# Batch order, one DMA per tensor and batch into 256-byte rows, and weights staged in the second batch's buffers, in a gated linear attention with a max-out layer

## Chip, cores, metric

One core of one Trainium2 chip. The metric is the device time of one execution in microseconds (us), lower is better. Executions of a program on one core carry a state: slow where the run is more than 1.5% above the fastest of the same kernel.

## The reference

```python
batch, n_heads, seq, head_dim = (4, 8, 768, 48)      # q, k, v, f_logit: float32
f = 1.0 / (1.0 + np.exp(-f_logit))
for t in range(S):
    state = f[:, :, t, :, None] * state + np.einsum('bhd,bhe->bhde', k[:, :, t], v[:, :, t])
    y[:, :, t] = np.einsum('bhd,bhde->bhe', q[:, :, t], state)
x = np.ascontiguousarray(y.transpose(0, 2, 1, 3)).reshape(B * S, H * D)     # 3072 x 384
h1 = x @ w1                                          # 384 x 1024
h2 = x @ w2
out = np.maximum(h1, h2) @ w_out                     # 1024 x 384
```

A head's row of 48 floats is 192 bytes in memory, and the rows of one head and batch follow each other. Whatever a load looks like, it is made of runs of 192 B on the memory side.

## The kernel before

A batch's 768 positions are cut into 6 chunks of 128, so there are 24 tiles (4 batches x 6 chunks), taken chunk by chunk: chunk 0 of all batches, then chunk 1, and so on. Four tiles make a group for the second layer. Work of step i is interleaved with "units" of the second layer: `u_d` (matmul d, then Relu) and `u_o` (matmul o, then the copy `ob` and the output DMA).

```python
loads = ctx.enter_context(tc.tile_pool(name="loads", bufs=5))
...
def load(i):
    c, b = divmod(i, B)
    sl = slice(c * C, (c + 1) * C)
    t = {}
    for name, src in (("f", f_logit), ("k", k), ("q", q), ("v", v)):
        t[name] = loads.tile([C, H, D], F32, name=f"{name}t", tag=f"{name}t")
        nc.sync.dma_start(out=t[name], in_=src[b, :, sl, :].rearrange("h p d -> p h d"))
    ld[i] = t
...
for i in range(3):
    load(i)
nc.sync.dma_start(out=w2_f, in_=...)      # 1.5 MB each
nc.sync.dma_start(out=wo_f, in_=...)
load(3)
nc.sync.dma_start(out=w1_f, in_=...)
load(4)
...
ob = work.tile([C, dm], F32, name="ob", tag="ob", bufs=3)
nc.vector.tensor_copy(ob, ps)
nc.sync.dma_start(out=out[r0:r0 + C, :], in_=ob)
...
for i in range(-4, T):
    if i >= 0:
        s_y(i)            # state and y of tile i
    unit()
    if 0 <= i + 2 < T:
        s_tr(i + 2)       # transposes of k', q', copy trs
    unit()
    if 0 <= i + 1 < T:
        s_a(i + 1)        # scores and mask (am)
    unit()
    if 0 <= i + 3 < T:
        s_cum(i + 3)      # cumulative log gates, exp, k' and q' on GpSimd
    unit()
    if i >= 0:
        s_xT(i)
    ...
    if i >= 0 and i % B == B - 1:
        push_group(i // B)
    if 0 <= i + 4 < T:
        s_ell(i + 4)      # reads f, casts v (vb)
    if 5 <= i + 8 < T:
        load(i + 8)
```

## Time and profile before

| | before |
|---|---|
| time, median of 2 runs | 186.99 us (186.93 to 187.04) |
| span of the profiled execution | 183.6 us |
| TensorE busy | 138.6 us (75%) |
| first d matmul of groups 0, 1, 2 | 59.22, 81.98, 104.27 us |
| DMA packets (page, part 3) | 105,154 |

How to read it: the span's last two thirds are set by TensorE, and the second layer's matmuls run in program order, so the starts of the groups' first d matmuls on TensorE's timeline tell where time was lost: each delay stays to the end. A timeline line gives start and length in us, engine, line, operation and tiles, and in brackets the engine's idle time before it with what ended it. A window line gives the stretch and its length, the busy us (and counts) of TensorE, its weight loads, VectorE, ScalarE and GpSimd, then the granted clock, the DMA share and GB/s. A packet is one piece of a DMA as the profile records it; where the DMA share is above 1, the records of one engine's packets overlap in time.

### The profile page before, as it was taken

The numbers are of one execution on the slowest core, as the hardware profiler recorded it, in microseconds if no ns is written. First come the engines' busy times: TensorE is split into PE (matmuls) and PEld (weight loads), VectorE is DVE, ScalarE is ACT, GpSimd is POOL, SyncE is SP. The second block draws the span as 40 slices with busy tenths as digits, with TensorE's granted clock in tenths as the row PEclk, the third lists the DMA queues.
The fourth block names the chain that finished last, engine by engine and source line by source line (L and its number), as shares of the span: only waits on it lengthen the run. The fifth ranks groups of instructions, "written<-read, shape, count | busy, mean of one in ns | idle before, by whom it ended". The sixth has DMA issues, their size and how long they took to land.

```text
span 183.6 us, 3633 instructions
## 1 busy us (share of the span) xinstructions
PE 138.6 (75%) x1373; PEld 85.4 (46%) x1384; DVE 102.5 (56%) x161; ACT 86.1 (47%) x200; POOL 75.7 (41%) x107
## 2 busy tenths in 40 slices
PE   0000208946778989999999998999899988998992
PEld 0000106534555545655456654665556654564560
DVE  8200605389777576686676676766776744452031
ACT  2000074483555675446744577346873376412700
POOL 8200004646666366544466544566544644000000
PEclk9999999985555999999999999999999999999999
DMA  6999999999999997698996999969801120022022
GB/s 114 194 185 347 373 199 362 186 187 171 194 189 190 164 191 131 165 209 174 195 151 164 215 172 186 172 142 216 152 0 43 50 86 0 4 87 86 0 89 86
DMA packets 105154, 28.56 MB, mean 156 GB/s; under 512 B 100272, under 2 KB 104368, under 8 KB 105136
## 3 DMA queue, kind: packets, MB, share of 16 engines
q1 hardware_dynamic: 105136, 28.32, 77.1%
q8 instruction: 11, 0.18, 0.5%
q14 instruction: 7, 0.06, 0.1%
HBM read 23.59 MB, written 4.72 MB: 154 GB/s over the span
## 4 chain that ended last, share of the span: by engine, by line
issue 39%; PE 32%; POOL 23%; ACT 3%; POOLq 1%; DVE 1%; ACTq 0%
PE o L172 13%; POOL qp L221 11%; POOL kp L220 9%; PE d L156 9%; PE tr L230 6%; PE a L245 2%; POOL st L98 1%; ACT ei L216 1%; PE y L272 1%; ACT ed L217 1%; PE y L277 1%; ACT gT L158 1%; POOLq L345 1%; POOL ell L94 0%; PE cum L208 0%
## 5 line engine op out<-in xcount | busy, mean ns | idle before, releaser
L220 POOL TENSOR_TENSOR kp<-kt,ei 128x384 bf16<-128x384 f32 x24 | 24.9, 1036 | 76.4 <-issue 38.9
L156 PE MATMUL d<-xT,wd 128*128 128x512 bf16 x133 | 36.7, 383 | 2.3 <-DVE xT L291 1.1
L158 ACT ACTIVATE gT<-d 128x512 bf16<-128x512 f32 x48 | 29.0, 605 | 19.0 <-PE d L156 18.5
L172 PE MATMUL o<-wo,gT 128*128 128x384 bf16 x192 | 37.7, 326 | 0.0
L234 DVE COPY trs<-tr 128x1024 bf16<-128x1024 bf16 x24 | 16.6, 692 | 25.8 <-PE tr L230 25.7
L248 DVE TENSOR_TENSOR am<-a,mask 128x1024 bf16<-128x1024 f32 x24 | 29.3, 1219 | 2.9 <-PE a L245 2.9
L216 ACT ACTIVATE ei<-cum 128x384 f32<-128x384 f32 x24 | 11.7, 489 | 38.2 <-PE cum L210 38.2
L221 POOL TENSOR_TENSOR qp<-qt,ed 128x384 bf16<-128x384 f32 x24 | 27.6, 1148 | 0.0
L176 DVE COPY ob<-o 128x384 f32<-128x384 f32 x24 | 13.4, 558 | 23.3 <-PE o L172 22.4
L172 PEld LDWEIGHTS <-gT 128*128 128x128 bf16 x192 | 17.8, 98 | 10.4
L267 POOL TENSOR_TENSOR st<-tmp,fl 64x192 bf16<-64x192 f32 x40 | 20.0, 501 | 2.3 <-DVE tmp L264 0.8
L124 PE MATMUL w2tp<-ident,w_h 128*128 128x128 bf16 x24 | 3.5, 308 | 21.0 <-DVE w_h L112 21.0
L201 DVE CAST vb<-vt 128x384 bf16<-128x384 f32 x24 | 16.9, 703 | 0.0
L156 PEld LDWEIGHTS <-wd 128*128 128x128 bf16 x144 | 11.8, 98 | 10.8 <-issue 2.3
L172 PE MATMUL o<-w2o,xT 128*128 128x384 bf16 x72 | 15.7, 327 | 0.0
L230 PE MATMUL tr<-ident,qp 128*128 128x128 bf16 x96 | 10.6, 239 | 5.8 <-POOL qp L221 5.0
L277 PE MATMUL y<-vb,am 128*128 128x48 bf16 x192 | 12.0, 190 | 2.2 <-DVE am L248 1.4
L116 ACT CAST wo<-wo_f 128x768 bf16<-128x768 f32 x4 | 3.1, 824 | 21.9 <-DMA wo_f<-in_moe_w_out_dram 21.9
L208 PE MATMUL cum<-ell,ut 128*128 128x384 bf16 x24 | 8.9, 369 | 6.0 <-ACT ell L199 6.0
L277 PEld LDWEIGHTS <-am 128*128 128x128 bf16 x192 | 10.3, 101 | 6.4 <-DVE xT L291 3.7
L280 ACT CAST x<-y 128x384 bf16<-128x384 f32 x24 | 11.2, 467 | 4.2 <-PE y L277 4.1
L199 ACT ACTIVATE ell<-e 128x384 bf16<-128x384 f32 x24 | 12.5, 523 | 0.9
(42 smaller groups left out, 185.1 us busy)
## 6 DMA issues: line engine op xcount, KB each, us to landing
ft<-in_f_logit_dram SPq DMA_DIRECT2D x24, 192.0 KB, 4.3
kt<-in_k_dram SPq DMA_DIRECT2D x24, 192.0 KB, 4.2
qt<-in_q_dram SPq DMA_DIRECT2D x24, 192.0 KB, 4.2
vt<-in_v_dram SPq DMA_DIRECT2D x24, 192.0 KB, 4.3
out_dram<-ob SPq DMA_DIRECT2D x24, 192.0 KB, 2.0
w_f<-in_moe_w_dram SPq DMA_DIRECT2D x2, 1536.0 KB, 7.7
wo_f<-in_moe_w_out_dram SPq DMA_DIRECT2D x1, 1536.0 KB, 11.0
```

The source lines that it names most:

```text
L156: nc.tensor.matmul(out=ps, lhsT=wd[:, j, f * C:(f + 1) * C], rhs=xT[:, j, :], start=(j == 0), stop=(j == JG - 1))
L158: nc.scalar.activation(gT[:, f, :], ps, AF.Relu)
L172: nc.tensor.matmul(out=ps, lhsT=mms[n][0], rhs=mms[n][1], start=(n == 0), stop=(n == len(mms) - 1))
L201: nc.vector.tensor_copy(vb, t["v"].rearrange("p h d -> p (h d)"))
L216: nc.scalar.activation(ei, ps[:, 0:dm], AF.Exp)
L220: nc.gpsimd.tensor_mul(kp[:, :, 0:D], t["k"], ei.rearrange("p (h d) -> p h d", h=H))
L221: nc.gpsimd.tensor_mul(qp[:, :, 0:D], t["q"], ed.rearrange("p (h d) -> p h d", h=H))
L230: nc.tensor.transpose(out=ps[:, n, p, :], in_=src[:, 2 * p:2 * p + 2, :].rearrange("p h d -> p (h d)"), identity=ident)
L234: nc.vector.tensor_copy(tr, ps)
L248: nc.vector.tensor_mul(am.rearrange("p o n c -> p (o n) c"), ps.rearrange("p o n c -> p (o n) c"), mask)
L267: nc.gpsimd.tensor_mul(new[r, :, e], tmp[r, :, e], s["fl"][r, :].unsqueeze(2).to_broadcast([DP, NP, D]))
L277: nc.tensor.matmul(out=y[:, ds], lhsT=am[:, o, p, :], rhs=vb[:, ds], start=(c == 0), stop=(c == 0 or o == 1))
```

## The change

Its intent: fewer and larger loads. Tiles go batch by batch. The first batch is still loaded tile by tile; from the second on, one DMA per tensor brings all six tiles (1.18 MB). Rows of 192 B are put every 256 B, which makes a buffer 12,288 B a partition, just what a weight matrix in float32 needs; so the three weight matrices are staged in the second batch's buffers.

```diff
-    loads = ctx.enter_context(tc.tile_pool(name="loads", bufs=5))
+    lb = {n: [consts.tile([C, H, nch, DP], F32, name=f"{n}b{x}") for x in range(2)] for n, _ in SRC}   # DP = 64
     def load(i):
-        c, b = divmod(i, B)
+        b, c = divmod(i, nch)
...
+            nc.sync.dma_start(out=lb[name][b % 2][:, :, c, 0:D],
+                              in_=src[b, :, sl, :].rearrange("h p d -> p h d"))
+    def load_batch(b, names):
+        for name, src in SRC:
+            if name in names:
+                nc.sync.dma_start(out=lb[name][b % 2][:, :, :, 0:D].rearrange("p h c d -> p (h c) d"),
+                                  in_=src[b].rearrange("h (c p) d -> p (h c) d", c=nch))
-    w1_f = consts.tile([C, JG, d_ff], F32, name="w1_f")
+    w1_f = lb["f"][1].rearrange("p h c d -> p (h c d)").rearrange("p (j f) -> p j f", j=JG)
     ... (w2_f in lb["k"][1], wo_f in lb["q"][1])
     load(4)
+    load(5)
...
-        if 5 <= i + 8 < T:
-            load(i + 8)
+        if i == 0:
+            load_batch(1, "fkqv")
+        if i >= 0 and i % nch == 1 and i // nch + 2 < B:
+            load_batch(i // nch + 2, "fv")
+        if i >= 0 and i % nch == 2 and i // nch + 2 < B:
+            load_batch(i // nch + 2, "kq")
```

The rest of the diff follows the new order of tiles in the state, the groups and the output rows.

More of the change, by code (lines that the diff above doesn't have):

```diff
@@ L54, with loaded @@
     nc.scalar.preload_act_table_set("natural_log_exp_and_others")
-    ld = {}
+    SRC = (("f", f_logit), ("k", k), ("q", q), ("v", v))
+    lb = {n: [consts.tile([C, H, nch, DP], F32, name=f"{n}b{x}") for x in range(2)] for n, _ in SRC}
     def load(i):
-        c, b = divmod(i, B)
+        b, c = divmod(i, nch)
         sl = slice(c * C, (c + 1) * C)
-        t = {}
-        for name, src in (("f", f_logit), ("k", k), ("q", q), ("v", v)):
-            t[name] = loads.tile([C, H, D], F32, name=f"{name}t", tag=f"{name}t")
-            nc.sync.dma_start(out=t[name], in_=src[b, :, sl, :].rearrange("h p d -> p h d"))
-        ld[i] = t
-    w1_f = consts.tile([C, JG, d_ff], F32, name="w1_f")
-    w2_f = consts.tile([C, JG, d_ff], F32, name="w2_f")
-    wo_f = consts.tile([C, FG, dm], F32, name="wo_f")
+        for name, src in SRC:
+            nc.sync.dma_start(out=lb[name][b % 2][:, :, c, 0:D],
+                              in_=src[b, :, sl, :].rearrange("h p d -> p h d"))
+    def load_batch(b, names):
+        for name, src in SRC:
+            if name in names:
+                nc.sync.dma_start(out=lb[name][b % 2][:, :, :, 0:D].rearrange("p h c d -> p (h c) d"),
+                                  in_=src[b].rearrange("h (c p) d -> p (h c) d", c=nch))
+    def loaded(i, name):
+        b, c = divmod(i, nch)
+        return lb[name][b % 2][:, :, c, 0:D]
+    w1_f = lb["f"][1].rearrange("p h c d -> p (h c d)").rearrange("p (j f) -> p j f", j=JG)
+    w2_f = lb["k"][1].rearrange("p h c d -> p (h c d)").rearrange("p (j f) -> p j f", j=JG)
+    wo_f = lb["q"][1].rearrange("p h c d -> p (h c d)").rearrange("p (j f) -> p j f", j=FG)
     for i in range(3):
@@ L176, in u_o @@
                 nc.vector.tensor_copy(ob, ps)
-                r0 = b * S + g * C
+                r0 = (g * B + b) * C
                 nc.sync.dma_start(out=out[r0:r0 + C, :], in_=ob)
@@ L194, in s_ell @@
     def s_ell(i):
-        t = ld[i]
+        b, c = divmod(i, nch)
+        t = {n: loaded(i, n) for n in "fkqv"}
         e = work.tile([C, dm], F32, name="e", tag="e")
         ell = ell_b[i % 2]
-        nc.scalar.activation(e, t["f"].rearrange("p h d -> p (h d)"), AF.Exp, scale=-1.0)
+        nc.scalar.activation(e.rearrange("p (h d) -> p h d", h=H), t["f"], AF.Exp, scale=-1.0)
         nc.scalar.activation(ell[:, :, 0:D], e.rearrange("p (h d) -> p h d", h=H), AF.Ln, bias=1.0)
         vb = work.tile([C, dm], BF16, name="vb", tag="vb", bufs=6)
-        nc.vector.tensor_copy(vb, t["v"].rearrange("p h d -> p (h d)"))
+        nc.vector.tensor_copy(vb.rearrange("p (h d) -> p h d", h=H), t["v"])
         st[i] = {"ell": ell, "v": vb}
     def s_cum(i):
-        s, t = st[i], ld[i]
+        b, c = divmod(i, nch)
+        s = st[i]
+        t = {n: loaded(i, n) for n in "fkqv"}
         ell = s["ell"]
@@ L222, in s_cum @@
         s.update(fl=fl, qp=qp, kp=kp)
-        del ld[i]
     def s_tr(i):
@@ L252, in s_y @@
     def s_y(i):
-        c, b = divmod(i, B)
+        b, c = divmod(i, nch)
         s = st[i]
@@ L283, in s_xT @@
     def s_xT(i):
-        c, b = divmod(i, B)
+        b, c = divmod(i, nch)
         s = st.pop(i)
-        if b == 0:
-            xT_g[c] = work.tile([C, JG, GT], BF16, name="xT", tag="xT", bufs=3)
+        g, n = divmod(i, B)
+        if n == 0:
+            xT_g[g] = work.tile([C, JG, GT], BF16, name="xT", tag="xT", bufs=3)
         ps = ps_s.tile([C, JG, C], BF16, name="xtp", tag="s")
@@ L290, in s_xT @@
             nc.tensor.transpose(out=ps[:, j, :], in_=s["x"][:, j * C:(j + 1) * C], identity=ident)
-        nc.vector.tensor_copy(xT_g[c][:, :, b * C:(b + 1) * C], ps)
+        nc.vector.tensor_copy(xT_g[g][:, :, n * C:(n + 1) * C], ps)
     for i in range(-4, T):
```

## The prediction

> **What bounds the kernel now.** I read the page's forty slices first, then a table of windows, then the timelines of single engines.
>
> ```profile
> PE   0000208946778989999999998999899988998992
> PEclk9999999985555999999999999999999999999999
> DMA  6999999999999997698996999969801120022022
> GB/s 114 194 185 347 373 199 362 186 187 171 194 189 190 164 191 131 165 209 174 195 151 164 215 172 186 172 142 216 152 0 43 50 86 0 4 87 86 0 89 86
> ```
>
> A slice is 4.6 us. Three stages show. Up to about 40 us the DMA engines are full and TensorE waits for weights and first tiles. From 40 to 60 us TensorE is half busy at half clock. From 60 us on it is at nine tenths, to the end. The DMA row is nearly full until about 130 us, which looks like a bound, but the windows (engine busy times, then granted clock, DMA share, GB/s) say otherwise:
>
> ```profile
> 5.00:10.00 5.00, 0.00 (x0) 0.00 (x0) 0.89 (x1) 0.00 (x0) 0.61 (x2) 1.00 1.31 192
> ...
> 45.00:50.00 5.00, 4.06 (x48) 3.01 (x47) 3.92 (x7) 2.73 (x9) 3.53 (x5) 0.50 1.01 190
> ...
> 85.00:90.00 5.00, 4.32 (x51) 2.53 (x50) 3.22 (x6) 4.12 (x10) 3.04 (x4) 1.00 1.17 196
> ...
> 135.00:140.00 5.00, 4.70 (x57) 2.93 (x55) 3.39 (x6) 3.21 (x8) 3.04 (x4) 1.00 0.00 0
> ```
>
> With no DMA at all (135 to 140 us) TensorE is as busy as with it. The q, k, v, f tiles move at about 190 GB/s wherever they move alone, so the four tiles of a step, 786,432 bytes, take 4.14 us, and a step takes longer: on VectorE's timeline the casts of v (vb) are 4.5 us apart from 45 to 54 us,
>
> ```profile
> 40.06 1.33 DVE L119 TENSOR_TENSOR wd<-w_f 128x1024 bf16<-128x1024 f32 x1
> ...
> 44.95 0.95 DVE L201 CAST vb<-vt 128x384 bf16<-128x384 f32 x1
> ...
> 49.46 0.95 DVE L201 CAST vb<-vt 128x384 bf16<-128x384 f32 x1
> ...
> 53.97 0.96 DVE L201 CAST vb<-vt 128x384 bf16<-128x384 f32 x1
> ```
>
> and later four steps take 22.3 us (output copies below: 72.89 to 95.17). So loads are hidden now. The 45-to-60 us stage is one latency loop (cum, exp, two GpSimd products, transpose); there is no projection work yet, for the first group of four tiles is pushed only after step 3. From its first d matmul (59.22 us on TensorE's timeline) TensorE sets the end: what delays that matmul delays the end by as much.
>
> **What the Trainium skill says.**
> 1. "DMA: Bandwidth & Descriptors", section "Why small descriptors are slow (HBM only)": each packet pays a fixed overhead. The trace agrees: the median packet takes 15 ns for 192 B, 65 ns for 1536 B, 159 ns for 4096 B, about 8 ns plus size. 192 B / 15 ns x 16 engines is 205 GB/s, near the 190 seen. The changed kernel moves the same 98,304 packets of 192 B.
> 2. The same page, "How a descriptor splits into AXI transactions": a start off a 256 B boundary costs beats. The new rows start on one in SBUF, not in HBM. The fit above already explains 15 ns without such a penalty, so I give alignment little.
> 3. The same page, "Why a DMA increments its semaphore by 16 and not by 1": only the full count says that all data has landed. So nobody can use the first tile of a batch DMA before its last has come. No trace of the kernel before can show it, since there each tile had a DMA of its own.
> 4. "TensorE: Matmul & The Clock Gate", Part 1: half clock after idle windows, full clock after about 3.4 us of sustained work. Agrees: 0.5 from 40 to 60 us, and full clock from 60.7 us, 1.5 us after dense work began.
>
> **The change, part by part.**
> *Fewer issues.* 96 input DMAs become 24 small and 12 of 1.18 MB. Issues run on SyncE's queue and are waited for by nobody but transfers; DMAs of 192 KB already stream at 190 GB/s. Gain: 0.
> *Order.* The six tiles of a batch follow each other, so the state of step i is needed in step i+1, not i+4. In the kernel before, in steady state, the state product ends at 106.37 us and the next step's first use is at 109.04 us: 2.7 us of slack. The same numbers of state products and y matmuls exist. Cost: 0.
> *Staging.* The weights' loads come in the same order at the start; load(5) is issued at the same place, now without waiting for a free buffer. Gain 0. But f of batch 1 goes where w1 lay, so in the built program its DMA waits for the last wd subtraction, which ends at 40.06 + 1.33 = 41.4 us. Before, the seventh tile was being issued from 36.9 us.
> *First stall.* Batch 1 comes as f, k, q, v, 4 x 1,179,648 B = 4.72 MB, at 190 GB/s 24.8 us. The shortest landing of a 192 KB tile is 2.7 us, of which 1.03 is transfer, so latency is 1.7 us. v lands at 41.4 + 1.7 + 24.8 = 67.9 us. Step 2 casts v of the seventh tile, at 53.97 us before: VectorE, in order, stands 13.9 us. Behind that cast it still has to do vb 0.35, tmp 0.55, trs 0.69, am 1.22, xT 0.35, then d starts: 71.3 us in place of 59.22. **Cost 12.1 us**, all on the path.
> *Clock.* The stall leaves TensorE cold; dense work then runs at half clock for 3 to 7 us in place of 1.5. About **1.5 us**.
> *Second stall.* Outputs share the queue with the batches and have three buffers (ob):
>
> ```profile
> 72.89 0.56 DVE L176 COPY ob<-o 128x384 f32<-128x384 f32 x1
> ...
> 81.11 0.56 DVE L176 COPY ob<-o 128x384 f32<-128x384 f32 x1 [0.80 <-PE o L172]
> ...
> 95.17 0.56 DVE L176 COPY ob<-o 128x384 f32<-128x384 f32 x1
> ...
> 103.40 0.56 DVE L176 COPY ob<-o 128x384 f32<-128x384 f32 x1 [0.80 <-PE o L172]
> 103.87 0.35 DVE L291 COPY xT<-xtp 128x384 bf16<-128x384 bf16 x1
> ```
>
> In the built program batch 3's four DMAs stand between outputs 4 and 5 on SyncE. In the old times, output 4 is copied at 81.11, f of batch 3 issues at 82.1, q lands 1.7 + 24.8 later at 108.6, output 5 behind it at about 109.2. Output 8, due at 103.40, reuses output 5's buffer, so VectorE waits 5.8 us, and behind it xT of step 11, which the next group's d needs. **Cost 5.8 us**, and about **1 us** of clock. For batch 2 the same sum just fits: it lands at 67.9 + 24.8 = 92.7, output 1 at 93.2, and output 4 is due at 81.11 + 13.6 = 94.7.
> Sum: 187.0 + 12.1 + 1.5 + 5.8 + 1.0 = 207.4; I say 207.
>
> **The rivals.**
> (a) *Aligned rows or large DMAs stream faster.* At 230 GB/s batch 1 needs 20.5 us: v at 63.6, d 7.8 us late, the second stall 1.5 us, clock 1.5: 198 us. For it: the skill's alignment section, and its advice of at least 1 MiB per DMA. Against: the packet fit, and 190 GB/s with small DMAs queued. At the 373 GB/s of the weights there would be almost no stall: 188 to 190.
> (b) *Only the first stall.* If output 5 slips past batch 3, or if f of batch 3 starts early: 200 to 201 us. For it: the ring's depth is not in the profile. Against: one queue, in order.
> (c) *The shorter state loop becomes the bound.* If GpSimd's products came late, each of 20 state steps could lose up to 1 us: up to 20 us more. Against: the slack of 2.7 us.
> (d) *Freed DMA time helps.* It cannot shorten a TensorE-bound second half: windows without DMA are no faster. About 187.
>
> **Range and chances.** 207 if both stalls come in full; (a) in part or (b) gives 198 to 201; slower transfers, with 5% less rate costing 1.3 us in each stall, or a colder clock, give 212. Range 198 to 212. Faster would need a gain that no view shows: 0.02. Within 2% needs nearly the weights' rate: 0.05. Slower: 0.93.
>
> **What would show it.** The DMA groups should list 24 small and 12 large loads, the large ones streaming at 185 to 195 GB/s; v of batch 1 landing near 68 us and VectorE's cast of it waiting some 14 us for that DMA; the first d near 71 us with PEclk at five tenths beyond 70; output 8's copy waiting some 6 us for an output DMA. From there steps of 5.6 us again. The prediction is wrong if the batches stream well above 190 GB/s, if no wait ends on v of batch 1, or if the steady step is not 5.6 us.

## The result, and the profile after

222.75 us (median of 2 runs, 222.57 to 222.92) against 186.99: slower, ratio 1.191 (95% interval 1.186 to 1.196). Ratios here are the mean time of one kernel's fast runs over that of the other's of the same rounds, so not quite the ratio of the medians quoted. The range of the prediction ended at 212: the direction was right, the size wrong.

The slices of the kernel after (5.5 us each):

```profile
PE   0000169468700088995699970689998999999893
PEclk9999999955555569999589995599999999999999
DMA  8999999979999999999599989200210012002012
GB/s 123 163 172 393 256 324 173 107 133 163 163 168 163 163 163 166 163 166 179 150 159 167 167 150 186 100 0 0 74 71 3 0 73 76 0 3 106 36 39 107
```

TensorE has three holes that were not there before, and each is followed by slices at half clock. The rate row is the surprise: where it read 185 to 195 before, it reads about 163, and it does so from the second slice on, while loads are still made tile by tile. The windows of the kernel after say the same (engine busy times, then granted clock, DMA share, GB/s):

```profile
5.00:10.00 5.00, 0.00 (x0) 0.00 (x0) 0.91 (x1) 0.00 (x0) 0.64 (x2) 1.00 1.53 164
...
65.00:70.00 5.00, 0.00 (x0) 0.00 (x0) 0.00 (x0) 0.00 (x0) 0.00 (x0) 0.50 0.94 165
...
85.00:90.00 5.00, 4.21 (x40) 2.08 (x39) 2.82 (x4) 3.89 (x9) 1.76 (x2) 1.00 1.06 166
...
150.00:155.00 5.00, 4.70 (x54) 2.89 (x52) 3.39 (x7) 3.06 (x8) 3.04 (x4) 1.00 0.00 0
```

From 65 to 70 us no engine works and the DMA engines move 165 GB/s: the core waits for data. From 150 us on it works as before.

VectorE's timeline after, the lines that answer to those of before (last wd subtraction, casts of v):

```profile
42.78 1.33 DVE L129 TENSOR_TENSOR wd<-fb,kb 128x1024 bf16<-128x1024 f32 x1
...
47.68 0.95 DVE L212 CAST vb<-vb 128x384 bf16<-128x384 f32 x1
...
52.19 0.95 DVE L212 CAST vb<-vb 128x384 bf16<-128x384 f32 x1
...
76.31 0.36 DVE L212 CAST vb<-vb 128x384 bf16<-128x384 f32 x1 [19.53 <-DMA vb<-in_v_dram]
```

The seventh tile's cast of v, at 53.97 us before, starts at 76.31 after a wait of 19.5 us for the batch's v: the predicted stall, larger. And the output copies:

```profile
105.70 0.56 DVE L186 COPY ob<-o 128x384 f32<-128x384 f32 x1 [4.86 <-DMA out_dram<-ob]
...
138.91 0.56 DVE L186 COPY ob<-o 128x384 f32<-128x384 f32 x1 [9.45 <-DMA out_dram<-ob]
139.38 0.35 DVE L304 COPY xT<-xtp 128x384 bf16<-128x384 bf16 x1
```

These are outputs 4 and 8. Each waits for a buffer whose output DMA stands behind batch loads on SyncE's queue (issue times; the last line is the first of the outputs behind q of batch 3):

```profile
106.84 0.71 SPq L70 DMA_DIRECT2D fb<-in_f_logit_dram  x1
108.00 6.01 SPq L70 DMA_DIRECT2D vb<-in_v_dram  x1
114.47 6.85 SPq L70 DMA_DIRECT2D kb<-in_k_dram  x1
121.77 7.80 SPq L70 DMA_DIRECT2D qb<-in_q_dram  x1
129.67 88.69 SPq L188 DMA_DIRECT2D out_dram<-ob  x20
```

The first d matmul of each group puts the loss in place. The lines of group 0 before, then of groups 0, 1 and 2 after, where TensorE itself waited 4.2 and 9.0 us for an xT copy behind a waiting output copy:

```profile
59.22 0.60 PE L156 MATMUL d<-xT,wd 128*128 128x512 bf16 x1
```
```profile
79.49 1.46 PE L166 MATMUL d<-xT,wd 128*128 128x512 bf16 x3
...
106.58 1.44 PE L166 MATMUL d<-xT,wd 128*128 128x512 bf16 x3 [4.17 <-DVE xT L304]
...
139.78 1.44 PE L166 MATMUL d<-xT,wd 128*128 128x512 bf16 x3 [8.96 <-DVE xT L304]
```

| first d of group | before | after | delay added since the last |
|---|---|---|---|
| 0 | 59.22 | 79.49 | 20.3 us |
| 1 | 81.98 | 106.58 | 4.3 us |
| 2 | 104.27 | 139.78 | 10.9 us |
| end of span | 183.6 | 220.8 | 1.7 us |

The sum is the 37.2 us between the spans.

What the loads are made of has changed too. Part 3 of the page, before:

```profile
DMA packets 105154, 28.56 MB, mean 156 GB/s; under 512 B 100272, under 2 KB 104368, under 8 KB 105136
```

and after:

```profile
DMA packets 48897, 28.54 MB, mean 129 GB/s; under 512 B 25584, under 2 KB 48112, under 8 KB 48880
```

The batch DMAs are recorded as 18,432 packets of 768 B, four rows each, where the tile loads have one packet a row. I had said the packets would stay the same.

### The profile page after: what moved, and what is told of

Same layout as the page of the kernel before. It is cut to its first block, busy times and chain, and to the rows that moved or that the text cites. A ratio compares the mean times of both kernels' runs of the same rounds, so it can differ in the third digit from the quotient of the medians.

```text
span 220.8 us, 3530 instructions
## 1 busy us (share of the span) xinstructions
PE 145.7 (66%) x1384; PEld 87.6 (40%) x1384; DVE 101.4 (46%) x161; ACT 86.5 (39%) x200; POOL 75.5 (34%) x107
## 3 DMA queue, kind: packets, MB, share of 16 engines
HBM read 23.59 MB, written 4.72 MB: 128 GB/s over the span
## 4 chain that ended last, share of the span: by engine, by line
PE 33%; issue 19%; DMA 17%; POOL 14%; SPq 10%; ACT 4%; DVE 2%; POOLq 0%; DVEq 0%; ACTq 0%
PE o L182 12%; PE d L166 11%; SPq L70 10%; DMA out_dram<-ob 9%; DMA vb<-in_v_dram 8%; POOL qp L234 6%; POOL kp L233 5%; PE tr L242 4%; PE a L257 3%; ACT ei L229 3%; POOL st L108 1%; ACT gT L168 1%; PE y L284 1%; DVE ob L186 1%; PE y L289 1%
## 5 line engine op out<-in xcount | busy, mean ns | idle before, releaser
L233 POOL TENSOR_TENSOR kp<-kb,ei 128x384 bf16<-128x384 f32 x24 | 24.9, 1039 | 84.7 <-ACT ei L229 76.4
L166 PE MATMUL d<-xT,wd 128*128 128x512 bf16 x144 | 41.6, 410 | 14.1 <-DVE xT L304 13.9
L234 POOL TENSOR_TENSOR qp<-qb,ed 128x384 bf16<-128x384 f32 x24 | 27.1, 1129 | 0.0
L212 DVE CAST vb<-vb 128x384 bf16<-128x384 f32 x24 | 15.8, 658 | 19.5 <-DMA vb<-in_v_dram 19.5
L166 PEld LDWEIGHTS <-wd 128*128 128x128 bf16 x144 | 12.4, 102 | 24.2 <-issue 16.4
L182 PEld LDWEIGHTS <-gT 128*128 128x128 bf16 x192 | 17.8, 97 | 10.4
L134 PE MATMUL w2tp<-ident,w_h 128*128 128x128 bf16 x24 | 3.5, 308 | 22.3 <-DVE w_h L122 22.3
L272 PE MATMUL sa<-vb,kp 128*128 128x96 bf16 x80 | 7.3, 220 | 16.3 <-DVE tmp L276 15.5
L242 PE MATMUL tr<-ident,qp 128*128 128x128 bf16 x96 | 11.3, 251 | 6.2 <-POOL qp L234 5.6
L209 ACT ACTIVATE e<-fb 128x384 f32<-128x384 f32 x24 | 13.0, 541 | 0.0
```

Of the source, the lines that this page charges most:

```text
L166: nc.tensor.matmul(out=ps, lhsT=wd[:, j, f * C:(f + 1) * C], rhs=xT[:, j, :], start=(j == 0), stop=(j == JG - 1))
L182: nc.tensor.matmul(out=ps, lhsT=mms[n][0], rhs=mms[n][1], start=(n == 0), stop=(n == len(mms) - 1))
L212: nc.vector.tensor_copy(vb.rearrange("p (h d) -> p h d", h=H), t["v"])
L233: nc.gpsimd.tensor_mul(kp[:, :, 0:D], t["k"], ei.rearrange("p (h d) -> p h d", h=H))
L234: nc.gpsimd.tensor_mul(qp[:, :, 0:D], t["q"], ed.rearrange("p (h d) -> p h d", h=H))
L242: nc.tensor.transpose(out=ps[:, n, p, :], in_=src[:, 2 * p:2 * p + 2, :].rearrange("p h d -> p (h d)"), identity=ident)
```

## The experiments

Twelve kernels ran, all correct. Each ran beside the kernel before on the same chip, whose medians in the four calls were 186.84, 186.03, 185.44 and 186.39 us.

The question: why 163 GB/s in place of 190, and is what remains just the two kinds of stall?

### a1_pitch48: no gaps between the rows

```diff
-    lb = {n: [consts.tile([C, H, nch, DP], ...)]}
+    lb_w = {n: [consts.tile([C, H * nch * DP], ...)]}               # the weights' views, as large as before
+    lb = ... lb_w[n][x][:, 0:H * nch * D] seen as [C, H, nch, D]    # rows every 192 B
```

> The changed kernel with the gaps taken out: rows of 192 B stand every 192 B in the batch buffers, so a batch DMA writes one contiguous 9216 B run per partition; everything else (order, batch DMAs, staging) as changed. Theory P (the gap between rows is what brought the load rate from 190 down to 163 GB/s): the batches stream at 190 GB/s or more, v of batch 1 lands near 44.2 + 1.7 + 24.8 = 70.7 us at the latest in place of 76.2, the output waits shrink from 14.3 us to about 6, and the time is 205 to 212 us. Theory Q (a DMA of a whole batch is slow by itself, whatever it writes to): still about 163 GB/s and 220 to 223 us.

206.32 us (203.96 to 207.29, 4 runs), ratio of fast runs 1.096 (1.083 to 1.108). The profiled run is a slow one (207.04), so I take from it only rates (from a5's below, slow too, rates and waits): 216 GB/s from 5 to 10 us, 212 from 50 to 55. So the batch DMA is not slow by itself; where its rows go decides.

### b1_pitch256, b2_pitch208, b3_order: one part each, in the kernel before

```diff
-        t[name] = loads.tile([C, H, D], F32, ...)
+        t[name] = loads.tile([C, H, 64], F32, ...)[:, :, 0:D]     # b1: rows every 256 B; b2: 52, every 208 B
```
```diff
-        c, b = divmod(i, B)                                       # b3, in load, s_y, s_xT, with the output rows
+        b, c = divmod(i, nch)
```

> The kernel before with one thing changed: its 96 tile loads write rows of 192 B every 256 B. Theory P: tiles move at about 163 GB/s in place of 190 from the first slice on (4.8 us a step, still less than the 5.6 us step, so hidden later); weights arrive about 2.7 us later, and the time is 189 to 191 us. Theory Q: 190 GB/s and 187 us as before.

> The kernel before with rows of 192 B every 208 B: a gap, but not the 256 B step. If any gap is what costs (the contiguous run of 1536 B a partition is broken up), 163 GB/s and 189 to 191 us as with 256 B. If it is the step of 256 B itself, 190 GB/s and 187 us.

> The kernel before with the order of tiles alone changed to batch by batch; 96 tile loads into five contiguous buffers as before. My theory: the state product has 2.7 us of slack before the next step's use, so 187 us, within 0.5%. Rival: the state loop of one step binds, each of 20 state steps loses up to 1 us, 190 to 205 us.

b1: 188.20 us, a little under the 189 to 191 expected, ratio 1.008 (1.001 to 1.014), and 163 GB/s in the first windows, one of them here:

```profile
5.00:10.00 5.00, 0.00 (x0) 0.00 (x0) 0.00 (x0) 0.00 (x0) 0.90 (x3) 1.00 1.51 163
```

b2: 186.83 us, ratio 1.001 (0.993 to 1.009), at 194 GB/s in the same window: a gap alone costs nothing, so my theory P of the gap fell. b3: 186.69 us, ratio 0.998 (0.990 to 1.007): the shorter state loop is free, as its 2.7 us of slack said, and the order is no part of the loss.

What tells b1 from b2? I looked up where the built programs put the buffers. They start 128 bytes past a multiple of 256 in the kernel after, and 160 past one in the kernel before and in b1. A row of 192 B that starts 128 past a boundary ends at 320: **every row of the "256-byte rows" crosses a 256 B boundary**, and so does every row of b1 (160 to 352). With rows every 192 B, before, the starts go round 160, 96, 32, 224, and three in four cross. In a1 one in two crosses, in b2 two in three (11 of 16 over its two kinds of buffers). The rates fall in that order. Hence theory X, crossings cost, against theory S, a step of 256 B is slow wherever it starts.

### a5_aligned, b4_aligned256, b5_start32: the same steps, shifted

```diff
+    pad = consts.tile([C, 32], F32, name='pad')                   # a5: 128 bytes; the batch buffers move to 0 past 256
     lb = {n: [consts.tile(...
```
```diff
-        ... loads.tile([C, H, 64], F32, ...)[:, :, 0:D]
+        ... loads.tile([C, H * 64 + 64], F32, ...)[:, 24:24 + H * 64] seen as [C, H, 64], [:, :, 0:D]   # b4; b5: 32:32 + H * 64
```

> The changed kernel with one 128-byte tile allocated ahead of the batch buffers. In the built program the eight buffers then start at 0 past a multiple of 256 B in place of 128, so no 192 B row crosses a 256 B boundary of SBUF any more, where in the changed kernel every row does (128 to 320). Theory X (crossings cost): so far the rate falls with the share of crossing rows: 216 to 227 GB/s at one half (a1), 190 at three quarters (before), 163 at all (after, b1, a3). At none I expect 240 to 330 GB/s, v of batch 1 by 59 to 65 us, no wait of an output copy above 1 us, and 189 to 196 us. Theory S (the step of 256 B is slow whatever the start, say because all rows fall on the same part of the memory): still 163 GB/s and 222 us.

> The kernel before with 96 tile loads into rows every 256 B, as b1_pitch256, but starting at 0 past a multiple of 256 B in place of 160: no row crosses. Theory X: 240 to 330 GB/s in the first 10 us in place of b1's 163 and before's 190; as loads are hidden later, only the start gains: 183 to 186 us. Theory S: 163 GB/s and 188 us, as b1.

> As b4_aligned256, but the rows start at 32 past a multiple of 256 B (32 to 224): no row starts on the boundary and none crosses one. If crossing is what costs, the rate of b4: 208 to 227 GB/s in the first 10 us, nearly all packets at 15 ns, 184 to 187 us. If a start off the boundary costs by itself, less: 163 to 195 GB/s.

Windows of b4, of b5, then of a5 (5 to 10 us, tile loads; 50 to 55 us, batch loads):

```profile
5.00:10.00 5.00, 0.00 (x0) 0.00 (x0) 0.89 (x1) 0.00 (x0) 0.61 (x2) 1.00 1.05 208
```
```profile
5.00:10.00 5.00, 0.00 (x0) 0.00 (x0) 0.91 (x1) 0.00 (x0) 0.63 (x2) 1.00 1.02 205
```
```profile
5.00:10.00 5.00, 0.00 (x0) 0.00 (x0) 0.90 (x1) 0.00 (x0) 0.62 (x2) 1.00 1.06 210
50.00:55.00 5.00, 4.11 (x49) 3.03 (x46) 2.81 (x5) 2.78 (x8) 3.52 (x6) 0.50 0.91 258
```

| rows that cross | kernels | tile loads, 5 to 10 us | batch loads, 50 to 55 us | median batch packet (768 B) |
|---|---|---|---|---|
| all | after, b1, a3 (below) | 164, 163, 164 GB/s | 163 GB/s (after) | 79 ns |
| 3 in 4 | before, b3 | 192, 189 | | |
| 11 in 16 | b2 | 194 | | |
| 1 in 2 | a1 | 216 | 212 | 47 ns |
| none | a5, b4, b5 | 210, 208, 205 | 258 (a5) | 42 ns |

Theory S is out: same step of 256 B, another start, 208 in place of 163 GB/s. The share of 192 B packets over 20 ns goes from 48% (b1) to 0.6% (b4, b5). The chip is not the cause, though b1 and b4 ran on different ones: on b4's chip, c1 (below), with rows as before, has 25% of such packets, and c3, with b4's rows, 0.7%. b5 starts no row on a boundary and still moves 205 GB/s: it is the crossing that costs; for a start off the boundary there is at most the small difference between b4 and b5. Tile loads gain nothing from one half to none: their packets then all take 15 ns, and 192 B / 15 ns x 16 engines is 205 GB/s. My expectation of 240 and more holds for the batches' larger packets alone.

In time: a5 is at 194.39 us (191.35 to 197.86), but three of its four runs count as slow, so there is no ratio; its one fast run is 191.35. By the medians, each set against the kernel before (35.8 and 9.0 us more), one 128-byte tile took some 27 us from the changed kernel. Its output wait, expected below 1 us, was 3.3 us in the profiled (slow) run. b4: 186.31 us, ratio 1.001 (0.994 to 1.007), b5: 186.30, ratio 1.003 (0.999 to 1.008): faster tile loads brought the kernel before nothing, not even the 1 to 4 us that I expected of the start for b4; its first d came at 59.85 us, no earlier than before's 59.22.

### a2_ob8: eight output buffers

```diff
-                ob = work.tile([C, dm], F32, name="ob", tag="ob", bufs=3)
+                ob = work.tile([C, dm], F32, name="ob", tag="ob", bufs=8)
```

> The changed kernel with eight output buffers in place of three. Theory: the two waits of VectorE's output copies for output DMAs that stand in the queue behind batch loads (4.9 and 9.5 us, 14.3 together) are on the path; they go, and with them most of two cold restarts: the time falls by 12 to 17 us, to 206 to 211 us, and the first d of group 1 starts near 102 us, that of group 2 near 125. Rival: these waits only take the place of waits that would come anyway (loads of batches 2 and 3 landing late); then less than 5 us is gained.

207.55 us, ratio 1.116 (1.108 to 1.124), all runs fast: 15.2 us less than after, or 14.2 with each set against the kernel before of its own call. VectorE's waits in a2, longest first; the 14.3 us for output DMAs, in two waits of up to 9.5 us, are gone and the one for v stays:

```profile
...
DVE ob L186 <- PE o L182: 22.1, 16, 7.2
DVE vb L212 <- DMA vb<-in_v_dram: 19.9, 1, 19.9
DVE w_h L122 <- DMA kb<-in_moe_w_dram: 15.1, 1, 15.1
```

First d of groups 0, 1, 2: 79.91, 104.36, 126.66 us. From group 0 to 1 it takes 24.45 us, where before took 22.76. I put these 1.7 us down to the cold clock after the first stall, which was at half until 85.2 us, 5.3 us after the first d (in the kernel before for 1.3 us); no run tests it apart. From 1 to 2 it takes 22.3, as before. So both output waits were on the path.

### a3_tile_loads: the changed kernel with tile loads throughout

```diff
         if i == 0:
-            load_batch(1, "fkqv")
-        ... (load_batch of 2 and 3)
+            load(6)
+            load(7)
+        if 8 <= i + 8 < T:
+            load(i + 8)
```

> The changed kernel with its buffers, gaps, order and staging, but batches 1 to 3 loaded tile by tile (72 more DMAs of 192 KB, issued eight steps ahead). Theory: what the batch DMAs cost is that the first tile of a batch is usable only with its last: here v of the seventh tile lands near 44.2 + 1.7 + 4.8 = 51 us, before step 2 needs it (56.7), outputs wait for at most a tile or two, and only the slower start (2.7 us) stays: 189 to 192 us. Rival: the rate of 163 GB/s or the staging in batch 1's buffers is the cost, and the time stays above 200 us.

189.42 us, ratio 1.020 (1.013 to 1.027), still at 163 GB/s with all rows crossing. So all that a3 keeps of the change (slow rate, order, staging, three output buffers with one wait of 2.3 us) costs 2%, of which the rate alone, by b1, is 0.8%, and the whole-batch DMAs cost the rest: they turn a rate that could have stayed hidden into waits.

### a7_mended: all three mends

```diff
+    pad = consts.tile([C, 32], F32, name='pad')
-                ob = work.tile(..., bufs=3)
+                ob = work.tile(..., bufs=8)
-            load_batch(1, "fkqv")
+            for j in range(nch, 2 * nch):
+                load(j)
```

> The change with three mends: the buffers start on a multiple of 256 B, eight output buffers, and batch 1 alone loaded tile by tile (batches 2 and 3 in one DMA per tensor). If nothing else in the change costs, no wait on v of batch 1 or on an output is left, steps are 5.6 us and the time is that of before, 184 to 188 us: large DMAs bring nothing, since loads were hidden already. If something else costs, it is above 189 us.

185.86 us, ratio 1.002 (0.996 to 1.008), and no wait of VectorE for v or for an output is left. Batches 2 and 3 still come in one DMA per tensor. The idea without its three costs is worth nothing here: loads were hidden.

### c1_weights_early, c3_weights_early_aligned: towards a better kernel

The slices show what does bind: the start. TensorE's first matmul waits for w2, which stands behind three tiles.

```diff
-    for i in range(3):
-        load(i)
+    load(0)
     nc.sync.dma_start(out=w2_f, ...)
     nc.sync.dma_start(out=wo_f, ...)
-    load(3)
+    load(1)
+    load(2)
     nc.sync.dma_start(out=w1_f, ...)
+    load(3)
     load(4)
```

> Towards a better kernel: before with w2 and w_out loaded straight after the first tile in place of after the third (8 DMAs later ones). The weights land 8 us earlier and with them the first transposes; the tiles behind them stay supplied at 190 GB/s. I expect the first d matmul 2 to 6 us earlier and 181 to 185 us; if the loads of tiles 1 and 2 then bind the start, 186 to 187.

> c1_weights_early and b4_aligned256 together: if both the order of the first loads and the crossings of rows bind the start, 2 to 5 us below c1 (177 to 182 us); if loads no longer bind it, the same as c1.

c1: 180.13 us (179.80 to 180.22), ratio 0.969 (0.965 to 0.973). TensorE's first instruction before, and in c1:

```profile
20.33 0.29 PE L124 MATMUL w2tp<-ident,w_h 128*128 128x128 bf16 x1 [20.33 <-DVE w_h L112]
```
```profile
12.30 0.29 PE L125 MATMUL w2tp<-ident,w_h 128*128 128x128 bf16 x1 [12.30 <-DVE w_h L113]
```

It comes 8.0 us earlier, the first d 7.2 us earlier (51.98), and the span is 5.2 us shorter (178.4): more than I expected. c3 (b4's rows as well) is at 179.70, ratio 0.968 (0.963 to 0.972), the same as c1: the rate of the loads does not bind even then. c1 is the better kernel, by nothing but the order of its first loads.

## Why the prediction was wrong

**What bounds: right.** TensorE sets the end from its first d on; delays of the first d of each group add up to the whole loss (37.2 us), and steps without a wait were as before. Two readings on the way were loose, and little rests on them. TensorE was not "half busy" from 40 to 60 us: the window shown has 4.06 of 5 us. And item 4's "Agrees" holds for the direction only: full clock came 1.3 to 1.5 us after the first d, not some 3.4, and from 45 to 50 us the clock stayed at half with TensorE that busy (the "3 to 7 us" at half clock came out as 2.2, 5.8 and 3.3 us after the three stalls).

**Fewer issues, order: right**, 0 us each (b3: 0.998; a7: 1.002).

**First stall: right in mechanism, 12.1 us predicted, 20.3 measured.** v of the batch was what VectorE waited for, in order. The terms: the DMA of f issued at 44.2 in place of 41.4 us (2.8 us), because the start's loads were slower (in a5, without crossings, it issued at 41.3); the 4.72 MB took 28.9 us at 163 GB/s in place of 24.8 (4.1 us); and the cast came 1.5 us later than 44.2 + 1.7 + 28.9. The landings in the trace settle this last: f landed 10.4 us after its issue, k, q and v each 7.2 to 7.3 us after the one before, so the first DMA took 3.2 us beyond its 7.2 us of transfer, where I had counted 1.7. (My 71.3 for the first d was 0.2 us more than its own terms, which give 71.1.)

**Clock after it: right in size in a2 only**, 1.5 predicted, 1.7 there. In the changed kernel full clock came back at 81.7 us, 2.2 us after the first d, and it cost little.

**Batch 2 and output 4: wrong.** "The same sum just fits" at 190 GB/s; at 163 output 4's copy waited 4.9 us and TensorE, behind it, 4.2 us, nearly all of the 4.3 us between groups 0 and 1.

**Second stall: right in mechanism, 5.8 + 1.0 predicted, 10.9 + 1.7 measured.** With 163 GB/s in its sum: f issues at 106.84, q lands 1.7 + 28.9 later at 137.4, output 5 at about 138 (in the trace 138.3 and 138.8), and the copy of output 8 began at 138.91. Of the 10.9 us TensorE's wait is 9.0; in the same stretch its clock was at half until 112.4 us, 5.8 us after the first d of group 1. That cold restart after output 4's wait was not in the prediction.

**The step that failed** is the second of the section on the skill: "The new rows start on one in SBUF" and "The fit above already explains 15 ns without such a penalty, so I give alignment little". Both halves were wrong. The rows did not start on a boundary: I took the 256 B step for alignment and did not look up the buffers' addresses, which were in the built program. And the fit used median packets of the whole run. In the kernel before 22% of the 192 B packets take over 20 ns, and their mean is 18.4 ns, not 15; from 5 to 10 us, where tiles move alone, the median is 18 ns (28 in b1, 15 in b4). The 190 GB/s that I took for the rate of a 192 B row was already that of rows of which three in four cross. In its place the runs showed 163 GB/s with every row crossing, where a7 and a5, without crossings, moved the batches at about 250. The page's account, that an unaligned descriptor costs more transactions, was the right lead. From it I drew a rival that could only be faster; the same page allowed slower. The miss of the packet count (768 B packets) worked the other way and could not show, since in the changed kernel four crossing rows made a packet of 79 ns, no better than four of 20. Rival (a) describes a5, where rows do not cross: its best run, 191.35 us, falls between its two figures.

**Shown and not shown.** That crossing 256 B of SBUF address costs, and how much, is shown by shifted buffers (b1 against b4 and b5, whose tiles are also 256 B longer; after against a5, where all later tiles move by 128 B too). The addresses are those of the built programs. On the memory side the rows' addresses are the same in every kernel, so no run tells what a crossing costs there. The cost is not in proportion to the share of crossing rows: in tile loads one half cost nothing. Why a crossing costs inside the DMA engine no run shows; that it is a second transaction is the page's account. What makes four rows share a packet is open too.

## What to carry to other kernels

A DMA as large as a whole batch is also a wait as long as a whole batch: before merging loads, ask when the first consumer needs its first piece, and what small transfers will stand behind the large one in the same queue. Row pitch is not alignment: look up the address at which the allocator put the buffer, and put short rows where none crosses a 256 B boundary. And judge a transfer's cost by its rate where it moves alone. The median packet hides the slow ones, and the mean overstates them where packets overlap: 192 B / 18.4 ns x 16 engines is 167 GB/s in the kernel before, less than the 190 measured.

## What the Trainium skill lacked or had wrong

- "DMA: Bandwidth & Descriptors", "How a descriptor splits into AXI transactions": right in direction. Its split gives a crossing row of 192 B a second transaction, but its words put the cost on a start off a 256 B boundary, tell of reads only and give no rate. Here, in writes to SBUF, rows that start 32 past a boundary and cross none moved at 205 GB/s, about as those on it (208), and rows that all cross at 163.
- The same page, "Rules for kernel authors", asks for at least 1 MiB per DMA and has no row on where short rows land in SBUF. DMAs of 1.18 MB of crossing 192 B rows gave 163 GB/s, less than the 192 of 192 KB DMAs before; 128 bytes of shift of the buffers brought them to 258.
- The same page, "Queues, rings and completion order", says that each engine takes a ring in order, and the trace agrees (an output landed 1.9 us after its issue alone, 10.9 us behind batch 2); no rule warns of small outputs queued behind large loads: 14.3 us of waits here, 14 to 15 us of time (a2).
- No page says when the rows of a DMA share a packet: one row a packet (192 B) in tile loads of 8 rows a partition, four (768 B) in batch loads of 48.
